# Tiles of x and pieces of the qkv weights in one packed array, and an order made with other costs of transfers

## The chip, the core and the metric

The kernel runs on one core of a Trainium2 chip. The metric is the time of one execution on the device in microseconds (us). Besides PE (TensorE: matmuls, and the loads of their stationary operand, PEld), the core has DVE (VectorE), ACT (ScalarE), POOL (GpSimd) and SP (SyncE), which here issues every DMA. Each engine runs its own list of instructions in the order in which it was built; an instruction that waits holds up all that stand behind it on its engine.

## What is computed

```python
def _A_ref(x, wqkv, wo):                      # linear attention, 32 heads of 16
    q, k, v = split_heads(x @ wqkv)
    phi = lambda t: where(t > 0, t + 1, exp(t)) + 1e-6
    pq, pk = phi(q), phi(k)
    kv = einsum("bhsd,bhse->bhde", pk, v)
    z = einsum("bhsd->bhd", pk)
    num = einsum("bhqd,bhde->bhqe", pq, kv)
    den = einsum("bhqd,bhd->bhq", pq, z)[..., None] + 1e-6
    return merge_heads(num / den) @ wo
def _B_ref(x, w_gate, w_up, w_down):
    return (gelu(x @ w_gate) * (x @ w_up)) @ w_down

xn = layernorm(x)
return x + _A_ref(xn, wqkv, wo) * silu(_B_ref(xn, w_gate, w_up, w_down))
```

x is 2048 tokens by 512, the inner width of the feed-forward part is 1792, everything is in 32-bit floats.

## The kernel before

A 32-bit product is made of three fast ones: each operand is split into a high part (a cast on ACT) and a low part (the difference, on DVE or POOL), and PE sums high x high, high x low and low x high (`sum3`, whose matmuls all carry line 506 in the profile; the splits carry 484 and 490). The large products use seven block products in place of eight, so sums of blocks are formed first, mostly on POOL.

The stages: up to 145 us, layer normalisation, q and k (`plain` for the first two pairs of tiles, then `first_products` and `rest`) and the sum G of xn by phi(k) (`gps`); then the feed-forward part for the second 1024 tokens, with the splits of all weights on the way (139 to 345 us); the small products that give one matrix per head; the feed-forward part for the first 1024 tokens, with the queries' normalisation in between (`queries`: tiles q, u, ptq, pT, then stored as pn_d); and from about 560 us the product S with these queries (read back as `pb`), the gate and the output.

**The start.** x comes in tiles of 128 tokens, 256 KB each, `x0`, `x4`, `x1`, `x5` and so on (`load_x`, L589), in a ring of four buffers. The array is row-major, so such a tile lies in one piece in memory. The weights of q, k and v lie as [3, 128, 4, 512]: a piece [1, :, k] of 256 KB is 128 rows of 2 KB, 8 KB apart. `wk1` and `wk2` are two pieces each of k's weights, `wq1` and `wq2` of q's, `wv` of v's. A tile of x gets statistics (`st`, L644; `mv`, L645; `ve`, L647, all DVE), the root on POOL (`rstd`, L649), the normalised tile (`xn`, L653, DVE), four transpositions on PE (`pt`, L675) and then on ACT a copy (`xt`) and the high parts `Xh` (L484); DVE makes `Xl`. The weights become `kq` (casts on ACT, low parts on DVE, for wk2 on POOL). PE starts with 13 warm-up matmuls, then the transposition of x0, then `k` products; `fill` are matmuls without use that stand in the order where PE might wait.

**What sets the order.** Every operation is recorded by `do` with its engine and a cost in microseconds; a DMA also with its size (`dma`, L458). `Plan` replays the record with these costs: it gives each transfer a time on one shared queue (its way there, its bytes by RATE, its landing), runs the engines against each other in 14 rounds, and each round takes the operations by the due times that the round before gave. The last round's order is what is built. So any cost that is changed can move instructions on all engines, while the set of instructions stays the same.

Eight DMAs can be under way at a time: a ninth waits until the first has landed, and so on.

Of the kernel before, what the change touches and what calls it, by code (L numbers as in the profile page):

```python
# [71 lines left out]
class Op:  # L72
    __slots__ = ("eng", "cost", "fn", "pre", "suc", "key", "name", "port", "kb", "n", "out", "use")


class Plan:

    RATE = 365.0
    TAIL = {"PE": 0.19, "ACT": 0.13, "DVE": 0.12, "POOL": 0.07, "SP": 0.0}
    HEAD = {"PE": 0.14, "ACT": 0.01, "DVE": 0.01, "POOL": 0.04, "SP": 0.05}  # L80
    SAME = {"ACT": 0.15, "DVE": 0.13, "POOL": 0.09}
    LAND = 1.3
    SLOW, FULL = 1.3, 6.0
    WAY = 0.45
    BEGIN = 0.65
    ROUNDS = 14
    MARGIN = (0.1, 0.12, 1.0)
# [7 lines left out]

    def do(self, eng, cost, fn, out, *ins, more=(), key=None, name="", kb=0):
# [7 lines left out]
        op.pre, op.suc, op.kb = set(), [], kb  # L104
# [36 lines left out]
    def hop(self, p, s):  # L141
        if p.eng == "SP":
            return self.LAND + (0.0 if s.eng == "SP" else self.HEAD[s.eng])
        if p.eng == s.eng:
            return self.SAME.get(p.eng, 0.0) if set(p.out) & set(s.use) else 0.0
        return self.TAIL[p.eng] + self.HEAD[s.eng]

    def link(self, pe_keys, to_pe, to_all, landing):
# [10 lines left out]
        self.behind = [[(p.n, lag(p, o)) for p in o.pre] for o in self.ops]  # L159
        self.info = [(o.eng, o.cost, o.port, o.kb / self.RATE) for o in self.ops]  # L160
        chain = [list(row) for row in self.ahead]
# [4 lines left out]
    def tails(self, nxt):  # L166
# [16 lines left out]
        for i in reversed(topo):  # L183
            _, cost, _, move = self.info[i]
            late[i] = min([late[j] - lag for j, lag in nxt[i]], default=0.0) - cost - move
        return late

    def run(self, nxt, late):
# [3 lines left out]
        for row in nxt:  # L192
            for j, _ in row:
                left[j] += 1
        free = dict.fromkeys(self.TAIL, self.BEGIN)
        coming = {e: [] for e in free}
        here = {e: [] for e in free}
# [5 lines left out]
        while len(done) < len(nxt):  # L203
# [30 lines left out]
            _, cost, lock, move = info[i]  # L234
            end, t = when + cost, when
# [30 lines left out]
    def replay(self, order):  # L266
# [5 lines left out]
        for i in order:  # L272
            queue[info[i][0]].append(i)
        free = dict.fromkeys(self.TAIL, 0.0)
        port = dma = last = 0.0
        n = 0
        while n < len(order):
# [9 lines left out]
            n += 1  # L287
            _, cost, lock, move = info[pick]
            start[pick] = when
# [3 lines left out]
            if eng == "SP":  # L293
                dma = max(dma, end + self.WAY)
                dma += move * (self.SLOW if dma < self.FULL else 1.0)
                end = dma
            last = max(last, end)
# [77 lines left out]
def kernel(  # L375
    ctx: ExitStack,
    tc: tile.TileContext,
    x: bass.AP,
    xt: bass.AP,
    wqkv: bass.AP,  # L380
    wo: bass.AP,
# [8 lines left out]
    nc = tc.nc  # L390
    S, D = x.shape
    DH = 16
# [64 lines left out]

    def dma(dst, src, kb, name=""):  # L458
        do("SP", 0.475, lambda o, i: nc.sync.dma_start(o, i), dst, src, kb=kb, name=name)

# [118 lines left out]

    tokens = [(8 * (n // 4) + n % 4, 8 * (n // 4) + 4 + n % 4) for n in range(NP)]  # L580

# [22 lines left out]
    for k in range(2):  # L604
        dma(half(wk1, k), ext(wqkv[1, :, k]), 256)
    for k in range(2):
        dma(half(wk2, k), ext(wqkv[1, :, 2 + k]), 256)
    load_next()
    load_next()
    for k in range(2):  # L610
        dma(half(wq1, k), ext(wqkv[0, :, k]), 256)
    for k in range(2):
        dma(half(wq2, k), ext(wqkv[0, :, 2 + k]), 256)
    for k in range(2):
# [139 lines left out]
    def q_out(v, t):  # L754
        dma(q_d(t, slice(t * P, (t + 1) * P)), phi(v, t, "q"), 256)

# [11 lines left out]
    def spill_x(n):  # L768
        for hl in "hl":
            dma(x_d[hl](n, (slice(None), slice(None), n)), xblock(hl, 0, 7, n).map(lambda ap: ap.bitcast(F32)), 896)  # L770

# [143 lines left out]
    for c in range(KT):  # L915
        g = U("p", range(18, 21), f"GTa{c}")
        copy("DVE" if c % 2 else "ACT", g, gps[c], D, "GT")
        dma(g_d(c, (slice(None), c)), g, 256)

# [44 lines left out]
    def keep_weights(key, ws):  # L964
        w_d[key] = []
        for g, w in enumerate(ws):
            n = GROUPS[g].stop - GROUPS[g].start
            d = dram_view([P, 2, n, P], f"{key[0]}{key[1]}{g}_d")(0, slice(None))
            dma(d, w.map(lambda ap: ap.bitcast(F32)), 128 * n)
            w_d[key].append(d)  # L970
# [19 lines left out]
    def prep_w(p, q):  # L990
# [5 lines left out]
        if p:  # L996
            u, i = divmod(q, 2)
            raw = D2(ring("raw", RAW), f"raw{q}", F32, (P, KT, 2 * P), 1)
            dma(raw, ext((w_up if i else w_gate)[u]), 512)
# [8 lines left out]
    def prep_d(p, u):  # L1008
        ws = wdn[p, u] = weights("D", u, f"wd{u}")
        if p:  # L1010
            raw = D2(ring("raw", RAW), f"draw{u}", F32, (P, 2, D), 1)
            dma(raw, ext(w_down[u]), 512)
            make_weights(ws, raw, D_BLOCKS, f"wd{u}")
# [125 lines left out]
    def queries(i):  # L1139
# [26 lines left out]
        j = t0 % 8  # L1166
        dma(pn_d[0 if t0 < 8 else 1](j // 2, (slice(None), slice(None), slice(j * P, (j + 2) * P))), pTs, 512)

# [34 lines left out]
    def attn_loads():  # L1203
# [73 lines left out]
    for n, key in enumerate(KEYS):  # L1277
        dma(g1_d(n, n), acc[1, key], 256)
    for a in range(2):
# [56 lines left out]
    def s_quad(p, c, forms, g, xp):  # L1336
# [12 lines left out]
        def block(dh, th, e, ps, to):  # L1349
# [14 lines left out]
            for h in range(m):  # L1364
# [4 lines left out]
                if not p:  # L1369
                    dma(ext(out[k * P:(k + 1) * P, lo:lo + w]), x, w // 2)  # L1370
            if p:
                left[k] = left.get(k, 2) - 1
                if not left[k]:
                    dma(ext(out[k * P:(k + 1) * P, HALF:2 * HALF]), o, 512)

# [19 lines left out]
    def x_again(p):  # L1395

        got = {}
        for k in (0, 2, 1, 3):
            got[k] = tile_in("dp", ring("br", BR), [P, HALF], F32, f"xp{p}{k}", 4)
            dma(got[k], ext(xt[k * P:(k + 1) * P, p * HALF:(p + 1) * HALF]), 512)  # L1400
        return got
# [29 lines left out]
def laid_out(inputs, shape):  # L1431
# [36 lines left out]
```

## Time and profile before

| | us |
|---|---|
| median of 3 runs (lowest, highest) | 605.5 (604.25, 607.61) |
| profiled execution | 608.37 |
| its span | 606.7 |
| PE busy in the span | 596.6 |
| DVE, POOL, ACT busy | 486.5, 353.1, 337.2 |

The profile is of one execution. Its span begins with the first and ends with the last instruction; 1.7 us of its time lie outside. Matmuls follow each other every 0.227 us (twelve in 2.72 us) but are shown 0.39 us long, since their ends overlap, so an idle PE shows, and a PE that runs at half clock shows only in the granted clock.

### The profile page before, as it was taken

Reading aid. Unit: us, or ns where it says so; the run is one execution under the profiler, and the core shown is the slowest. Engines: PE = TensorE matmul, PEld = TensorE weight load, DVE = VectorE, ACT = ScalarE, POOL = GpSimd, SP = SyncE. Lnnn points to the kernel's source line nnn. Section 1 sums busy time; section 2 is a strip of 40 time slices with the busy share of each in tenths; the row PEclk is TensorE's granted clock in tenths of the full one; section 3 lists DMA queues with packets and bytes.
Section 4 is the critical chain, followed back from the end, with each engine's and each line's share of the span. In section 5 each row is a group of like instructions: output and inputs, shape, how many; then the busy total and the mean of one; then the engine's idle time right before and its main releaser. Section 6 shows DMA issues by size and latency. Waiting matters only on the chain.

```text
span 606.7 us, 8238 instructions
## 1 busy us (share of the span) xinstructions
PE 596.6 (98%) x2696; PEld 490.5 (81%) x2696; DVE 486.5 (80%) x700; ACT 337.2 (56%) x610; POOL 353.1 (58%) x298
## 2 busy tenths in 40 slices
PE   7999999999999999999999999999999999999996
PEld 6888888888888888888887878888888888887875
DVE  5898888976598988998979764668865795689997
ACT  5767777786576744665365154645403540477831
POOL 4713854464487975996587234547604670658455
PEclk9999999999999999999999999999999999999999
DMA  7267811219849746973659979988639774899546
GB/s 242 78 209 232 281 70 58 94 54 352 324 149 328 245 180 229 352 256 123 231 177 382 377 231 413 408 285 294 203 126 316 256 240 142 311 298 335 180 139 242
DMA packets 58794, 143.14 MB, mean 236 GB/s; under 512 B 5504, under 2 KB 17024, under 8 KB 58752
## 3 DMA queue, kind: packets, MB, share of 16 engines
q1 hardware_dynamic: 58752, 142.63, 67.0%
q8 instruction: 21, 0.34, 0.3%
q14 instruction: 21, 0.17, 0.1%
HBM read 81.00 MB, written 61.60 MB: 235 GB/s over the span
## 4 chain that ended last, share of the span: by engine, by line
PE 92%; DMA 4%; DVE 3%; ACT 1%; issue 0%; SPq 0%; DVEq 0%; ACTq 0%
PE FX L506 24%; PE FZ L506 12%; PE DX L506 12%; PE gps L506 7%; PE FY L506 6%; PE DZ L506 6%; PE X L506 5%; PE SX L506 4%; PE Z L506 3%; PE DY L506 3%; PE SZ L506 2%; PE k L506 2%; PE q L506 2%; DMA pb<-pn_d 2%; PE Y L506 1%; PE ptq L1163 1%
## 5 line engine op out<-in xcount | busy, mean ns | idle before, releaser
L506 PE MATMUL FX<-Xh,w 128*128 128x512 f32 x448 | 151.7, 390 | 0.0
L1071 POOL TENSOR_TENSOR h<-h,g 128x512 f32<-128x512 f32 x42 | 64.5, 1540 | 92.3 <-DVE h L490 88.5
L506 PEld LDWEIGHTS FX<-Xh,w 128*128 128x128 f32 x448 | 83.9, 188 | 17.3
L490 POOL TENSOR_TENSOR h<-h,h 128x512 f32<-128x512 f32 x56 | 84.2, 1504 | 13.5 <-DVE hf4l L490 3.4
L506 PE MATMUL FX<-Xl,w 128*128 128x512 f32 x224 | 87.3, 390 | 0.0
L506 PE MATMUL FZ<-Xh,w 128*128 128x512 f32 x224 | 78.2, 391 | 0.0
L484 ACT COPY fu<-FX 128x512 f32<-128x512 f32 x56 | 32.9, 588 | 72.3 <-PE FX L506 60.5
L506 PE MATMUL gps<-pks,xns 128*128 128x512 f32 x192 | 49.4, 390 | 0.0
L506 PEld LDWEIGHTS FX<-Xl,w 128*128 128x128 f32 x224 | 42.0, 188 | 8.8
L506 PEld LDWEIGHTS FZ<-Xh,w 128*128 128x128 f32 x224 | 41.7, 188 | 8.7
L751 POOL TENSOR_TENSOR zacc<-zacc,kp 128x512 f32<-128x512 f32 x16 | 24.1, 1507 | 38.8 <-DVE kp L740 38.3
L1097 DVE TENSOR_TENSOR acc<-acc,DX 128x512 f32<-128x512 f32 x48 | 32.5, 683 | 14.8 <-PE DX L506 14.5
L506 PE MATMUL FZ<-Xl,w 128*128 128x512 f32 x112 | 43.7, 390 | 0.0
L506 PEld LDWEIGHTS gps<-pks,xns 128*128 128x128 f32 x192 | 36.0, 188 | 7.6
L506 PE MATMUL FY<-Xh,w 128*128 128x512 f32 x112 | 39.5, 393 | 0.0
L1097 DVE TENSOR_TENSOR acc<-acc,DZ 128x512 f32<-128x512 f32 x32 | 21.8, 681 | 12.6 <-PE DZ L506 8.8
L506 PE MATMUL X<-kq,Xh 128*128 128x512 f32 x96 | 31.1, 398 | 0.0
L490 DVE TENSOR_TENSOR h<-fu,FZ 128x512 f32<-128x512 f32 x28 | 19.2, 684 | 14.8 <-ACT fu L484 8.5
L1063 ACT ACTIVATE g<-g 128x512 f32<-128x512 f32 x42 | 26.6, 632 | 7.7 <-DVE g L490 7.5
L490 DVE TENSOR_TENSOR w<-raw,w 128x512 fp32r<-128x512 f32 (+1 forms) x28 | 24.9, 892 | 3.9 <-ACT w L484 3.9
L490 POOL TENSOR_TENSOR u<-q,zacc 128x512 f32<-128x512 f32 x16 | 22.2, 1404 | 9.8 <-DMA q<-q_d 9.8
L484 ACT COPY fe<-FX 128x512 f32<-128x512 f32 x28 | 16.4, 587 | 20.3 <-PE FX L506 17.0
(422 smaller groups left out, 1604.7 us busy)
## 6 DMA issues: line engine op xcount, KB each, us to landing
w_d<-w SPq DMA_DIRECT2D x36, 512.0 KB, 5.1
w<-w_d SPq DMA_DIRECT2D x36, 512.0 KB, 4.8
wd_d<-wd SPq DMA_DIRECT2D x21, 512.0 KB, 5.0
wd<-wd_d SPq DMA_DIRECT2D x21, 512.0 KB, 6.6
x<-in_x SPq DMA_DIRECT2D x16, 256.0 KB, 5.0
q_d<-qp SPq DMA_DIRECT2D x16, 256.0 KB, 2.0
q<-q_d SPq DMA_DIRECT2D x16, 256.0 KB, 4.3
pn_d<-pT SPq DMA_DIRECT2D x8, 512.0 KB, 6.4
```

The lines of the kernel that those rows point to most:

```text
L484: do("ACT", act(n), lambda o, i: nc.scalar.copy(o, i), dst, src, name=name)
L490: do(eng, c, lambda o, p, q: getattr(e, f"tensor_{op}")(o, p, q), dst, a, b, name=name)
L506: nc.tensor.matmul(o, v[i], v[i + 1], start=start and part == 0 and i == 0, stop=stop and part == 1 and i == len(v) - 2, skip_group_check=on)
L751: do("POOL", pool(D), lambda o, i: nc.gpsimd.tensor_add(o, o, i), zacc, p0, name="zacc")
L1063: curved("gelu", do("ACT", curve(NC), lambda o, i: nc.scalar.activation(o, i, AF.Gelu_apprx_tanh), g, ps if e is None else g, name="gelu"))
L1071: do("POOL", pool(NC), lambda o, i: nc.gpsimd.tensor_mul(o, o, i), h, g, name="h")
L1097: do("DVE", dve(NC), lambda o, i: nc.vector.tensor_add(o, o, i), a, ps, name="acc")
L1163: nc.tensor.transpose(o[:, k, :], a[:, k * P:(k + 1) * P], b)
```

## The change

The host stacks the sixteen tiles of x and the twelve pieces of wq, wk and wv into one array `in_first` of [28, 128, 512], each piece in one stretch of 256 KB, in the order FIRST: x0, wk1's two, x4, wk2's two, x1, x5, the four of q, the other tiles of x, the four of v. The kernel loads piece PLACE of it where it loaded from `in_x` or `in_wqkv`. Sizes, buffers and the count of DMAs stay.

The costs of transfers in `Plan` are replaced: in place of one way (0.45) and landing (1.3), RATE 365 and a factor of 1.3 in the first 6 us, there are four kinds with a way, a landing and a gap that is added to the transfer's time, and RATE 400. The kind "first" is given to the loads of the other weights and of x's transposed copy, "store" and "pieces" to stores. SP begins at 0.85 in place of 0.65. By that all engines get another order.

```diff
+PAIRED = [(8 * (n // 4) + n % 4, 8 * (n // 4) + 4 + n % 4) for n in range(8)]
+XS = [t for pair in PAIRED for t in pair]
+FIRST = [XS[0], ("k", 0), ("k", 1), XS[1], ("k", 2), ("k", 3), XS[2], XS[3], *[("q", k) for k in range(4)], *XS[4:], *[("v", k) for k in range(4)]]
+PLACE = {v: i for i, v in enumerate(FIRST)}
...
-    RATE = 365.0
+    RATE = 400.0
+    MOVES = {"load": (0.72, 0.8, 0.0), "first": (0.72, 0.8, 0.7), "store": (0.45, 0.43, 0.0), "pieces": (0.45, 0.43, 0.6)}
-    LAND = 1.3
-    SLOW, FULL = 1.3, 6.0
-    WAY = 0.45
     BEGIN = 0.65
+    ISSUE = 0.85
...
+        op.way, op.land, gap = self.MOVES[kind]
+        op.kb = kb / self.RATE + gap if kb else 0.0
...
         if p.eng == "SP":
-            return self.LAND + (0.0 if s.eng == "SP" else self.HEAD[s.eng])
+            return p.land + (0.0 if s.eng == "SP" else self.HEAD[s.eng])
...
             if eng == "SP":
-                dma = max(dma, end + self.WAY)
-                dma += move * (self.SLOW if dma < self.FULL else 1.0)
-                end = dma
+                end = dma = max(dma, end + way) + move
...
-        dma(xs[t], ext(x[t * P:(t + 1) * P, :]), 256)
+        dma(xs[t], ext(first[PLACE[t]]), 256)
...
-        dma(half(wk1, k), ext(wqkv[1, :, k]), 256)
+        dma(half(wk1, k), ext(first[PLACE["k", k]]), 256)
...
-            dma(half(wv[c // 2], c % 2), ext(wqkv[2, :, c]), 256)
+            dma(half(wv[c // 2], c % 2), ext(first[PLACE["v", c]]), 256)
...
+    def piece(v):
+        if isinstance(v, tuple):
+            c = d * "qkv".index(v[0])
+            return wqkv[v[1] * P:(v[1] + 1) * P, c:c + d]
+        return x[v * P:(v + 1) * P]
     arrays = {
-        "in_x": x,
+        "in_first": np.stack([piece(v) for v in FIRST]),
...
-        "in_wqkv": wqkv.reshape(d // P, P, 3, d).transpose(2, 1, 0, 3),
```

**ACT at the start**, before: the first instructions behind the load of its table. (pt0 is the transposition of x0, pt4 that of x4, a21 a high part of wq1.)

```order
L484 CAST kq0_221<-wk1_182 128x512 x2
L484 CAST xns0_233<-xn0_223 128x512
L484 COPY xt0_245<-pt0_235 128x512
L484 CAST Xh0_253<-pt0_235 128x256
L484 CAST kq0_221<-wk2_201 128x512
L484 CAST Xh0_253<-pt0_235 128x256
L484 CAST kq0_221<-wk2_201 128x512
L484 CAST a2100_273<-wq1_210 128x512
L484 CAST xns4_283<-xn4_275 128x512
L484 COPY xt0_245<-pt4_285 128x512
```

The same place now:

```order
L486 CAST kq0_216<-wk1_194 128x512 x2
L486 CAST xns0_232<-xn0_222 128x512
L486 CAST kq0_216<-wk2_201 128x512
L486 COPY xt0_251<-pt0_238 128x512
L486 CAST Xh0_255<-pt0_238 128x256 x2
L486 CAST kq0_216<-wk2_201 128x512
L486 CAST a2100_269<-wq1_214 128x512
L486 CAST a2101_277<-wq1_214 128x512
L486 CAST xns4_288<-xn4_281 128x512
L486 COPY xt0_251<-pt4_291 128x512
```

The cast of wk2's first piece moved ahead of the copy and of both casts of x0's transposition, and the cast of wq1's second piece ahead of xns4.

**DVE at the start**, before: from the statistics of x4 to the root's argument for x1 and x5.

```order
L644 BN_STATS st4_240<-x4_199 128x6
...
L490 TENSOR_TENSOR kq0_221<-wk1_182,kq0_221 128x512
L490 TENSOR_TENSOR Xl0_265<-pt0_235,Xh0_253 128x256
L644 BN_STATS st1_267<-x1_204 128x6
L653 TENSOR_SCALAR xn4_275<-x4_199,mv4_248,rstd4_257 128x512
L644 BN_STATS st5_279<-x5_208 128x6
...
L647 TENSOR_SCALAR ve1_299<-mv1_293 128x2
```

The same place now:

```order
L646 BN_STATS st4_234<-x4_199 128x6
...
L492 TENSOR_TENSOR kq0_216<-wk1_194,kq0_216 128x512
L646 BN_STATS st1_259<-x1_206 128x6
L492 TENSOR_TENSOR Xl0_267<-pt0_238,Xh0_255 128x256
L646 BN_STATS st5_271<-x5_208 128x6
...
L655 TENSOR_SCALAR xn4_281<-x4_199,mv4_245,rstd4_257 128x512
...
L646 BN_STATS st2_296<-x2_230 128x6
L647 BN_AGGR mv2_301<-st2_296 128x2
L649 TENSOR_SCALAR ve1_305<-mv1_279 128x2
```

The statistics of x1 and x5 moved ahead of Xl0 and xn4, and those of x2 ahead of ve1.

**ACT where the feed-forward part ends** and S begins, before: pT6 is the last transposition of the queries, stored as pn_d and loaded again as pb; hf0h are high parts of the last unit, which PE needs for DX and DZ.

```order
L484 COPY fu3_1_5236<-FX1_5128 128x512
L484 CAST Xh0_253<-pb100_5192 128x512
L484 COPY pT6_5201<-ptq7_5182 128x4x128
L476 ACT_TABLE_LOAD
...
L484 CAST hf0h_5216<-h12_1_5278 128x512
L1130 ACTIVATE g1_5_5274<-g1_5_5274 128x512
L484 CAST Xh0_253<-pb110_5297 128x512
L484 CAST hf0h_5216<-h22_1_5246 128x512
L484 CAST hf0h_5216<-h21_1_5262 128x512
```

The same place now:

```order
L486 COPY pT6_5222<-ptq7_5200 128x4x128
L486 COPY fu3_1_5237<-FX1_5126 128x512
L486 CAST Xh0_255<-pb100_5214 128x512
...
L486 CAST Xh0_255<-pb110_5269 128x512
L1132 ACTIVATE g1_5_5264<-g1_5_5264 128x512
L486 CAST hf0h_5216<-h12_1_5277 128x512
L1132 ACTIVATE g1_6_5288<-g1_6_5288 128x512
L486 CAST hf0h_5216<-h22_1_5247 128x512
L1132 ACTIVATE g1_7_5307<-g1_7_5307 128x512
L486 CAST hf0h_5216<-h21_1_5271 128x512
```

The copy of pT6 moved two places up, and the cast of pb110 ahead of the cast of h12. On PE the last product, a half of X before, is Z now.

More of the change, by code (lines that the diff above doesn't have):

```diff
@@ L94, in __init__, with do @@
         self.first = 0
-    def do(self, eng, cost, fn, out, *ins, more=(), key=None, name="", kb=0):
+    def do(self, eng, cost, fn, out, *ins, more=(), key=None, name="", kb=0, kind="load"):
         op = Op()
@@ L195, in run @@
         free = dict.fromkeys(self.TAIL, self.BEGIN)
+        free["SP"] = self.ISSUE
         coming = {e: [] for e in free}
@@ L233, in run @@
                 continue
-            _, cost, lock, move = info[i]
+            _, cost, lock, move, way = info[i]
             end, t = when + cost, when
@@ L274, in replay @@
         free = dict.fromkeys(self.TAIL, 0.0)
+        free["SP"] = self.ISSUE
         port = dma = last = 0.0
@@ L287, in replay @@
             n += 1
-            _, cost, lock, move = info[pick]
+            _, cost, lock, move, way = info[pick]
             start[pick] = when
@@ L293, in replay @@
             if eng == "SP":
-                dma = max(dma, end + self.WAY)
-                dma += move * (self.SLOW if dma < self.FULL else 1.0)
-                end = dma
+                end = dma = max(dma, end + way) + move
             last = max(last, end)
@@ L377 @@
     tc: tile.TileContext,
-    x: bass.AP,
+    first: bass.AP,
     xt: bass.AP,
-    wqkv: bass.AP,
     wo: bass.AP,
@@ L578, in kq_split @@
                 split(kq(slot, 0, i), kq(slot, 1, i), raw[:, i], D, f"kq{slot}", eng)
-    tokens = [(8 * (n // 4) + n % 4, 8 * (n // 4) + 4 + n % 4) for n in range(NP)]
+    tokens = PAIRED
     def half(v, i):
@@ L604 @@
     for k in range(2):
-        dma(half(wk1, k), ext(wqkv[1, :, k]), 256)
+        dma(half(wk1, k), ext(first[PLACE["k", k]]), 256)
     for k in range(2):
-        dma(half(wk2, k), ext(wqkv[1, :, 2 + k]), 256)
+        dma(half(wk2, k), ext(first[PLACE["k", 2 + k]]), 256)
     load_next()
@@ L610 @@
     for k in range(2):
-        dma(half(wq1, k), ext(wqkv[0, :, k]), 256)
+        dma(half(wq1, k), ext(first[PLACE["q", k]]), 256)
     for k in range(2):
-        dma(half(wq2, k), ext(wqkv[0, :, 2 + k]), 256)
+        dma(half(wq2, k), ext(first[PLACE["q", 2 + k]]), 256)
     for k in range(2):
@@ L1166, in queries @@
         j = t0 % 8
[L1167 removed]
+        dma(pn_d[0 if t0 < 8 else 1](j // 2, (slice(None), slice(None), slice(j * P, (j + 2) * P))), pTs, 512, "pieces")
     PAIRS = {2: [0], 3: [1], 4: [2], 5: [], 6: [], 7: [3], 8: [4], 9: [5], 10: [], 11: [6], 12: [7]}
@@ L1277 @@
     for n, key in enumerate(KEYS):
-        dma(g1_d(n, n), acc[1, key], 256)
+        dma(g1_d(n, n), acc[1, key], 256, "store")
     for a in range(2):
@@ L1369, in block @@
                 if not p:
-                    dma(ext(out[k * P:(k + 1) * P, lo:lo + w]), x, w // 2)
+                    dma(ext(out[k * P:(k + 1) * P, lo:lo + w]), x, w // 2, "store")
             if p:
@@ L1373, in block @@
                 if not left[k]:
-                    dma(ext(out[k * P:(k + 1) * P, HALF:2 * HALF]), o, 512)
+                    dma(ext(out[k * P:(k + 1) * P, HALF:2 * HALF]), o, 512, "store")
         left = {}
```

28 lines of the change are left out of this document (14 added, 14 removed).

## The prediction

> **What bounds the kernel now.** I read the page's busy table and then the windows: start and end of a stretch, its length, busy time of PE, PE's weight loads, DVE, ACT and POOL (with instruction counts), the granted PE clock, the DMA share and GB/s.
>
> ```profile
> PE 596.6 (98%) x2696; PEld 490.5 (81%) x2696; DVE 486.5 (80%) x700; ACT 337.2 (56%) x610; POOL 353.1 (58%) x298
> ```
> ```profile
> 0.00:15.00 15.00, 11.17 (x54) 9.74 (x55) 8.75 (x21) 7.92 (x15) 6.01 (x12) 0.95 0.72 245
> 15.00:30.00 15.00, 14.94 (x72) 12.35 (x71) 12.54 (x23) 11.27 (x22) 12.10 (x12) 0.94 0.24 72
> 30.00:45.00 15.00, 15.00 (x70) 12.35 (x70) 14.39 (x26) 10.45 (x17) 2.69 (x2) 1.00 0.64 211
> ...
> 315.00:330.00 15.00, 14.60 (x65) 11.71 (x64) 13.82 (x17) 7.43 (x15) 11.70 (x10) 1.00 0.99 364
> 330.00:345.00 15.00, 14.99 (x72) 12.25 (x71) 12.78 (x21) 4.01 (x7) 6.83 (x7) 1.00 1.03 405
> ...
> 540.00:555.00 15.00, 14.32 (x64) 11.43 (x63) 12.94 (x16) 9.39 (x17) 13.85 (x9) 1.00 0.97 328
> ```
>
> PE is the bound. Of the span of 606.7 us it is idle for 10.1: 3.83 in the first 15 us, 0.06 in the next, 0.40, 0.01 and 0.68 in the three late stretches shown, and the rest, 5.1, behind the last matmul. The matmuls themselves are not touched, so only four things can move: the start, the clock in it, the two small holes, and the end. The first is the largest, so I read it in order of time (start, duration, engine, line, operation, and in brackets the wait before it and what ended it).
>
> ```profile
> 3.55 0.70 DVE L644 BATCH_NORM_STATS2 st<-x 128x6 f32<-128x512 f32 x1 [2.45 <-DMA x<-in_x]
> 4.99 0.62 ACT L484 CAST kq<-wk 128x512 fp32r<-128x512 f32 x1 [2.91 <-DMA wk<-in_wqkv]
> 6.74 0.62 ACT L484 CAST kq<-wk 128x512 fp32r<-128x512 f32 x1 [1.14 <-DMA wk<-in_wqkv]
> 7.46 0.69 DVE L644 BATCH_NORM_STATS2 st<-x 128x6 f32<-128x512 f32 x1 [0.98 <-DMA x<-in_x]
> 9.28 0.62 ACT L484 CAST kq<-wk 128x512 fp32r<-128x512 f32 x1 [0.64 <-DMA wk<-in_wqkv]
> 9.98 2.51 POOL L490 TENSOR_TENSOR kq<-wk,kq 128x512 fp32r<-128x512 f32 x2 [0.38 <-DMA wk<-in_wqkv]
> 11.99 0.62 ACT L484 CAST a<-wq 128x512 fp32r<-128x512 f32 x1 [1.29 <-DMA wq<-in_wqkv]
> ```
>
> Each row starts when its tile lands, so these are the landings of x0, both pieces of wk1, x4, both pieces of wk2, and the first of wq1 (x1 and x5 lie between the last two). The steps are 1.44, 1.75, 0.72, 1.82, 0.70 and 2.01 us; the last is for three tiles, 0.67 each. Every tile has 256 KB, so three of the steps hold an extra 0.8 to 1.1 us, about 3 us together, and all three are steps to a wk piece. The windows show the same hole in the traffic:
>
> ```profile
> 2.50:3.50 1.00, 1.00 (x7) 1.00 (x7) 0.00 (x0) 0.00 (x0) 0.00 (x0) 1.00 0.90 342
> 3.50:5.00 1.50, 1.50 (x9) 1.50 (x9) 1.03 (x3) 0.01 (x1) 0.27 (x1) 1.00 0.50 119
> ...
> 8.50:12.00 3.50, 1.92 (x6) 0.97 (x6) 2.46 (x5) 1.56 (x5) 2.98 (x3) 1.00 1.04 396
> 9.75:13.25 3.50, 1.38 (x8) 0.91 (x8) 3.03 (x4) 2.01 (x5) 2.51 (x2) 1.00 0.79 301
> 13.25:16.75 3.50, 3.50 (x13) 2.82 (x11) 3.42 (x10) 2.11 (x6) 2.47 (x4) 0.52 0.28 85
> ```
>
> 342 GB/s, then 119 for 1.5 us with the transfer engines half busy; from 8.5 us on 396. The last two rows show the second loss: PE works 1.38 of 3.50 us, and in the next 3.50 us its clock is 0.52, which costs 0.48 x 3.50 = 1.7 us. What PE waited for is here:
>
> ```profile
> 6.73 0.60 PE L675 MATMUL pt<-ident,xn 128*128 128x128 f32 x4
> 8.27 0.37 ACT L484 CAST Xh<-pt 128x256 fp32r<-128x256 f32 x1
> 8.64 0.96 POOL L649 TENSOR_TENSOR rstd<-ve,neg_half 128x1 f32<-128x1 f32 x1 [3.35 <-DVE ve L647]
> 9.81 0.37 ACT L484 CAST Xh<-pt 128x256 fp32r<-128x256 f32 x1
> 11.26 1.52 DVE L653 TENSOR_SCALAR xn<-x,mv,rstd 128x512 f32<-128x512 f32 x1
> 12.83 0.44 PE L675 MATMUL pt<-ident,xn 128*128 128x128 f32 x2 [1.18 <-DVE xn L653]
> 16.23 1.82 PE L506 MATMUL k<-kq,b 128*128 128x512 f32 x6
> 17.89 0.60 PE L675 MATMUL pt<-ident,xn 128*128 128x128 f32 x4
> ```
>
> **The change, part by part.** *Packing.* It removes no bytes and no DMA: the first twelve tiles stay 256 KB each, issued by SP in nearly the same order. What can change is the spacing. Upper end: nothing, the hole belongs to the first microseconds of any traffic. Lower end: every step is 0.67 us. For the first speaks that the wq pieces, cut with the same stride, run in the 396 GB/s row. For the second speaks that all three long steps end in wk, the first pieces of in_wqkv to be read, while x4, 1 MB further on in the array that x0 had opened, comes in 0.72: the hole looks like the price of opening a second array, and the packed array is opened once, by x0. I take the second. Landings are then 3.55 + n x 0.68: wk1 at 4.2 and 4.9, x4 5.6, wk2 6.3 and 7.0, x1 7.6, x5 8.3, wq1 9.0, three microseconds before 11.99.
>
> The Trainium skill speaks against this: Perfetto Trace Analysis, section "Contiguity and DMAs", says that contiguity matters for a transfer only within a partition's line. The lines are 2 KB before and after, so by that rule packing gives nothing (the first rival). The 396 GB/s row agrees with it; the 119 GB/s row it does not explain.
>
> *The start, with these landings and the new order.* PE's first transposition stays at 6.73, since the 13 warm-up matmuls in front of it remain. ACT now casts wk2's first piece before it empties that transposition: ready at 6.3, cast by 7.0, hidden under the transposition, which ends at 7.33. (With wk2 at 9.28 this same move would hold both Xh casts to about 10.2.) The first k product starts at 8.3 in place of 8.69. Behind it stands x4's path, one step after the other: its statistics follow the split of the first wk piece on DVE, 6.4; POOL's rstd 7.5 to 8.4 in place of 8.64 to 9.60; POOL's two wk2 splits 8.4 to 10.9 (2.51) in place of 9.98 to 12.49. The normalisation xn took 1.52 us and ended 0.29 behind POOL's pair, though x0's took 0.55, so I let it end behind that pair again: 11.2 in place of 12.78. Second transposition: 11.25 in place of 12.83, **term A, -1.6 us**.
>
> From there to the row at 16.23 PE had 3.40 us for four transpositions, six products and a fill, about 2.0 us of work at full clock. If PE's idle share is small enough for the clock to hold, that stretch and the one behind it get back the 1.7 us. By the walk above PE works about 1.8 of the 3.5 us in front of 11.7 (six products and a transposition), against 1.38 of 3.50. Ends: 0 and -1.7. I take **term B, -1.3 us**, nearer to the full gain, since the share rises from 39% to some 50%. The third transposition, at 17.89 in the row, then comes at about 15.0. It needs the statistics of x1 and x5 only, but DVE's new order puts x2's statistics in front: x2 lands at about 11.0, in time.
>
> The Trainium skill, TensorE: Matmul & The Clock Gate, Part 1, has a free-running activity window of about 3.4 us after which an idle PE is halved. The 3.50 us at 0.52 agree; by a free-running window the same start can come out with or without the loss, which is the reason for B's ends.
>
> Does PE keep the 2.9 us? DVE is at 14.39 of 15 us from 30 to 45, so it must come forward too. Its xn of x4 ends 1.6 earlier, and in the stretch from 15 to 30 it is idle for 2.46, most of it behind the slow PE. That covers 2.9.
>
> *The order elsewhere.* From 30 to 315 us PE stands still nowhere. The hole at 540 to 555 is one place:
>
> ```profile
> 548.17 0.62 ACT L484 CAST hf0h<-h 128x512 fp32r<-128x512 f32 x1 [0.23 <-POOL h L490]
> ...
> 550.40 0.62 ACT L484 CAST Xh<-pb 128x512 fp32r<-128x512 f32 x1 [1.07 <-DMA pb<-pn_d]
> 551.60 0.73 PE L506 MATMUL DX<-hf0h,wd 128*128 128x512 f32 x2 [0.68 <-ACT hf0h L484]
> ```
>
> ACT stands at the cast of a loaded tile, two hf0h casts are queued behind it, and PE waits for them. In the new order ACT empties the last transposition of p two instructions earlier, so the store and the load behind it start earlier; but this cast has moved up in front of three hf0h casts. Ends: -0.8 (the hole is gone) and +2.7 (the cast at 548.17, which ran 2.2 us before it, now stands behind it). I take 0, nearest to the row as it is. wv, also packed now, is read at 315 to 340, where PE loses 0.4 us to other things: 0.
>
> *The end.* The last product was half of X, now it is Z. Behind it DVE has three 512-wide operations in place of two and two half ones:
>
> ```profile
> 602.39 0.69 DVE L490 TENSOR_TENSOR xp<-xp,SZ 128x512 f32<-128x512 f32 x1
> 602.99 0.42 DVE L490 TENSOR_TENSOR SX<-acc,SX 128x256 f32<-128x256 f32 x1
> 603.45 0.42 DVE L490 TENSOR_TENSOR xp<-xp,SX 128x256 f32<-128x256 f32 x1
> ```
>
> From Z's last matmul, now 0.8 later, three at about 0.7 end at the same 603.9; the last store has 256 KB, not 128. Ends -0.3 and +0.5; I take 0.
>
> **Sum.** -1.6 - 1.3 = -2.9 us. The profiled execution goes from 608.37 to 605.5 (span 603.8); it lies 2.9 above the median of the runs, 605.5, so the runs go to **602.6**.
>
> **Rivals.** *First: the pieces land as before.* For it: wq with the same stride is fast, and the hole could be the cold start of the queue. Against it: x4's short step. Then neither A nor B comes, and DVE's and ACT's heads wait for x1, x2 and wk2 somewhat longer: 605.5 to 606.5. *Second, slower: ACT's head at 548 to 551.* If the third pb pair lands after about 548.2, when that cast used to run, everything later goes to PE one for one: at the old 550.3 +2.7 us; with the next pair, which stands behind it on the same queue, about +4, and without the gain at the start 609. Against it: the earlier store. *Third: more comes back.* The clock holds entirely, the hole at 550 goes, and the waits of DVE behind 17 us go: -1.6 - 1.7 - 0.8 - 0.5 = -4.6, 600.9.
>
> **How the numbers follow.** Forecast 60%, its own range 600.8 to 604.5; first rival 22%, second 10%, third 8%. 0.5% is 3.0 us, about what a measurement of this kernel can tell from no change; the forecast lies just on that border, so I split it 31 to 29. Faster 31 + 8 = 39%; slower 8 of the second and 1 of the first = 9%; no difference 52%. The range for 8 in 10 leaves out the end of the third and most of the second: 600.0 to 607.0.
>
> **What would show it.** Right: wk2's first piece is cast near 6.5, not 9.28; no window between 3.5 and 8 us under 300 GB/s; the second transposition near 11.3; PE clock 1.00 throughout; the row at 16.23 near 13.5. Wrong at packing: long steps to the wk pieces again. Wrong at A: the wk2 splits on POOL start at 8.4 but xn does not end near 11.2. Wrong at B: a stretch at 0.5 in spite of it. Wrong at "elsewhere": PE idle above 1.5 us between 30 and 600, above all at 548 to 556.

## The result, and the profile after

The changed kernel is slower. The prediction was 602.6 us, within 600.0 to 607.0.

| | before | changed |
|---|---|---|
| median of 7 runs each, us | 605.75 (604.25 to 607.61) | 610.26 (608.78 to 612.88) |
| ratio to before, 95% interval | | 1.0072 (1.0047 to 1.0098) |
| profiled execution, its span | 608.37, 606.7 | 612.25, 610.5 |
| PE busy in the span | 596.6 | 597.8 |

The start came out nearly as forecast, and more than that was lost later. In the order of time, the first casts of weights, POOL's pair of wk2 splits, the second transposition, the row that stood at 16.23 and the third transposition, from the timeline of the changed kernel (start, duration, engine, line, operation, the wait before it and what ended it; lines are two higher than before):

```profile
4.31 0.62 ACT L486 CAST kq<-wk 128x512 fp32r<-128x512 f32 x1 [2.23 <-DMA wk<-in_first]
5.12 0.62 ACT L486 CAST kq<-wk 128x512 fp32r<-128x512 f32 x1 [0.20 <-DMA wk<-in_first]
7.12 0.62 ACT L486 CAST kq<-wk 128x512 fp32r<-128x512 f32 x1 [0.46 <-DMA wk<-in_first]
...
8.63 2.52 POOL L492 TENSOR_TENSOR kq<-wk,kq 128x512 fp32r<-128x512 f32 x2
11.50 0.66 PE L677 MATMUL pt<-ident,xn 128*128 128x128 f32 x4 [1.08 <-DVE xn L655]
13.61 1.54 PE L508 MATMUL k<-kq,b 128*128 128x512 f32 x6
15.19 0.66 PE L677 MATMUL pt<-ident,xn 128*128 128x128 f32 x4
```

And the windows of the changed kernel, with the columns of the prediction (stretch, length, PE, PEld, DVE, ACT, POOL busy, granted clock, DMA share, GB/s):

```profile
3.50:5.00 1.50, 1.50 (x9) 1.50 (x9) 1.03 (x3) 0.62 (x1) 0.14 (x1) 1.00 0.93 309
0.00:15.00 15.00, 12.61 (x62) 10.81 (x62) 10.39 (x25) 9.94 (x19) 7.05 (x14) 1.00 0.74 245
15.00:30.00 15.00, 14.90 (x75) 12.37 (x75) 14.25 (x26) 10.92 (x22) 13.08 (x11) 1.00 0.31 97
330.00:345.00 15.00, 12.71 (x60) 10.70 (x59) 9.72 (x15) 1.76 (x4) 3.60 (x5) 0.89 0.92 359
375.00:390.00 15.00, 13.60 (x64) 11.04 (x64) 9.02 (x12) 5.32 (x10) 8.40 (x7) 1.00 1.02 407
390.00:405.00 15.00, 14.66 (x64) 11.42 (x64) 12.20 (x20) 8.97 (x17) 5.36 (x4) 1.00 0.93 340
405.00:420.00 15.00, 14.61 (x72) 11.99 (x70) 8.97 (x13) 7.79 (x14) 9.31 (x7) 1.00 0.82 274
```

The hole of 119 GB/s is gone, PE works 1.4 us more in the first 15 us and keeps its clock: the third transposition comes 2.70 us earlier. The loss is in two places in which the kernel before had no such wait: 330 to 345 us, where PE is idle for 2.29 us and then has a lower clock, and 375 to 420 us, idle for 2.13, where PE of the kernel before was busy for all of the 45 us. What PE waited for, in the same timeline:

```profile
337.63 0.38 PE L1250 MATMUL pkv<-GT,wv 128*128 128x128 f32 x2
338.68 0.49 PE L1250 MATMUL pkv<-GT,wv 128*128 128x128 f32 x2 [0.67 <-DMA GT<-g_d]
340.68 5.37 PE L1250 MATMUL pkv<-GT,wv 128*128 128x128 f32 x28 [1.51 <-DMA wv<-in_first]
...
387.04 0.66 PE L1165 MATMUL ptq<-ident,q 128*128 128x128 f32 x4 [1.40 <-DVE q L1159]
```

`pkv` are the 32 kv products: per head, GT (the sum G) by wv. In the kernel before they ran without a wait:

```profile
343.84 3.73 PE L1248 MATMUL pkv<-GT,wv 128*128 128x128 f32 x32
```

They now take from 337.63 to 346.05, 8.42 us in place of 3.73: 4.7 us. The loads of wv did not get slower (median from issue to landing 7.4 us, 7.5 before); those of GT took 0.9 us more (9.7, 8.8 before). The second pair of wv was issued 3.1 us earlier than before (first the row of the kernel before, then of the changed one), but the products stand 6.2 us earlier:

```profile
335.47 0.93 SPq L459 DMA_DIRECT2D wv<-in_wqkv  x2
```
```profile
332.33 0.96 SPq L461 DMA_DIRECT2D wv<-in_first  x2
```

About half of the 6.2 us is that PE arrives earlier, the other half is the new order: by the count of PE's matmuls in front of the first product (in brackets behind PE's busy time), 1525 stood there and now 1512, 13 fewer, and 13 x 0.227 = 3.0 us. First the kernel before, then the changed one:

```profile
0.00:343.83 343.83, 339.53 (x1525) 280.43 (x1526) 291.62 (x426) 217.09 (x398) 218.94 (x202) 1.00 0.61 217
```
```profile
0.00:337.62 337.62, 335.09 (x1512) 276.69 (x1513) 286.31 (x419) 216.03 (x398) 220.52 (x202) 1.00 0.61 217
```

At 387 us it is the same on a longer path: the queries' transposition waits for DVE, DVE for POOL, and POOL for the load of q, issued 3.6 us later than before (372.18, was 368.60), while PE gets there 0.9 us later (385.64, was 384.70). First the transposition in the kernel before, without a wait, then the load and POOL in the changed one:

```profile
384.70 0.60 PE L1163 MATMUL ptq<-ident,q 128*128 128x128 f32 x4
```

```profile
372.18 1.08 SPq L461 DMA_DIRECT2D q<-q_d  x2
...
381.29 2.54 POOL L492 TENSOR_TENSOR u<-q,zacc 128x512 f32<-128x512 f32 x2 [7.16 <-DMA q<-q_d]
```

The hole at 548 to 556 us that the prediction watched became no larger: 0.68 us of idle PE before, 0.41 now. The end, from the start of the last matmul to the end of the span, went from 5.4 to 5.7 us.

### The profile page after: what moved, and what is told of

Same layout as the page of the kernel before. It is cut to its first block, busy times and chain, and to the rows that moved or that the text cites. A ratio compares the mean times of both kernels' runs of the same rounds, so it can differ in the third digit from the quotient of the medians.

```text
span 610.5 us, 8231 instructions
## 1 busy us (share of the span) xinstructions
PE 597.8 (98%) x2696; PEld 490.8 (80%) x2696; DVE 483.3 (79%) x700; ACT 335.6 (55%) x610; POOL 354.0 (58%) x298
## 4 chain that ended last, share of the span: by engine, by line
PE 80%; DMA 10%; DVE 5%; POOL 2%; ACT 1%; issue 1%; SPq 0%; POOLq 0%; DVEq 0%; ACTq 0%
PE FX L508 21%; PE DX L508 11%; PE FZ L508 10%; PE gps L508 7%; PE X L508 5%; PE DZ L508 5%; PE FY L508 5%; PE Z L508 3%; DMA q<-q_d 2%; PE DY L508 2%; PE SX L508 2%; PE q L508 2%; DMA GT<-g_d 2%; DMA x<-in_first 1%; DMA wv<-in_first 1%; PE Y L508 1%
## 5 line engine op out<-in xcount | busy, mean ns | idle before, releaser
L492 DVE TENSOR_TENSOR g<-fu,FZ 128x512 f32<-128x512 f32 x28 | 19.0, 680 | 8.9 <-ACT fu L486 4.0
```

Of the source, the lines that this page charges most:

```text
L492: do(eng, c, lambda o, p, q: getattr(e, f"tensor_{op}")(o, p, q), dst, a, b, name=name)
```

## The experiments

Each comparison has its own runs of the kernel before beside it, so ratios are compared, and not medians. A percent is 6.1 us.

### The two halves apart

`e1_pack` is the kernel before with the packed array; the planner's costs, and so every engine's order, are the old ones.

```diff
-        dma(xs[t], ext(x[t * P:(t + 1) * P, :]), 256)
+        dma(xs[t], ext(first[PLACE[t]]), 256)
...
-        dma(half(wk1, k), ext(wqkv[1, :, k]), 256)
+        dma(half(wk1, k), ext(first[PLACE["k", k]]), 256)
...
```

> The packed array alone; the costs of transfers in the planner, and so the order of every engine, are those of the kernel before. Theory A (the two halves of the change add: packing gives the start, the order takes it away elsewhere): the pieces land every 0.7 us as in the changed kernel, the third transposition (17.89 us before) comes near 15.5, no wait at the kv products, PE idle from 30 to 600 us stays near 1.1 us: 2 to 2.7 us less than before, 603.0 to 603.8 against 605.75. Rival B (what is gained at the start is given back, since PE then reaches the kv products earlier than their wv pieces can land, the transfers from 312 to 345 us being the limit): a wait of 1 to 3 us for wv at about 341 us, and a time of 605 to 606. Rival C (the fast landings need the new order of the loads too): the landings are as before and the time within 0.5 us of it.

Measured: 604.49 us against 606.31, ratio 0.9972 (0.9954 to 0.9990). `e2_order` is the other half: the changed kernel with the old arrays.

```diff
-        dma(xs[t], ext(first[PLACE[t]]), 256)
+        dma(xs[t], ext(x[t * P:(t + 1) * P, :]), 256)
...
```

> The new costs of transfers alone, with x and the qkv weights in their old two arrays; every engine has the order of the changed kernel. Theory A: all of the loss (some 6.5 us) and none of the gain at the start, and the wk2 cast that now stands ahead of the Xh casts waits for its late piece, up to 1 us more: 612 to 613.5 against 610.3 of the changed kernel and 605.75 before; the wait for wv ahead of the kv products is 1 to 2.5 us. Rival B (the loss comes from arriving early): PE comes 2.7 us later to the kv products, their wait for wv is gone, and the time is 607 to 609. Rival C (the gain at the start came with the new order of the loads): the start is as in the changed kernel, 610.

Measured: 613.54 us against 606.31, ratio 1.0123 (1.0091 to 1.0155). In its timeline both faults of the order are there, and one that packing may have covered: PE's first k product waits for Xh and starts at 9.78 us, 1.1 later than in the kernel before (8.69). The cast of wk2's late piece now stands ahead of Xh on ACT, with a wait of 0.36 us and 0.62 of work, which fits; but a second execution of the kernel before, in its old order, starts this product at 9.30, so the cause is not shown.

```profile
9.78 0.97 PE L509 MATMUL k<-kq,Xh 128*128 128x512 f32 x3 [2.37 <-ACT Xh L487]
...
340.45 0.49 PE L1251 MATMUL pkv<-GT,wv 128*128 128x128 f32 x2 [0.56 <-DMA GT<-g_d]
342.46 3.74 PE L1251 MATMUL pkv<-GT,wv 128*128 128x128 f32 x28 [1.51 <-DMA wv<-in_wqkv]
```

Theory A holds, though both times lie above its ranges, `e1_pack` by 0.7 us. Rival C falls: the first wk1 piece is cast at 4.29 us in `e1_pack`, in the old order, and at 5.01 in `e2_order`. Rival B falls: packing alone has no wait at the kv products, though PE reaches them at 340.99 and not at 343.84, and the order alone loses with the late start too. Packing is worth 0.28% with the old order (1.7 us, a little less than expected) and 0.51% with the new one (1.0123 less 1.0072); by the intervals these two do not differ. The order costs 1.0% with packed arrays (1.0072 less 0.9972, 6.1 us), 1.2% without.

### Which cost moved the kv products

`e3_rate` is the changed kernel with one constant put back.

```diff
-    RATE = 400.0
+    RATE = 365.0
```

> The changed kernel with one constant put back: RATE 365 in place of 400; the packed array, the kinds and their landings stay as changed. Theory A, as to which constant: a planner that believes in 400 has the last wv piece landed some 4 us ahead of when it does, and puts the kv products 3.4 us of PE work earlier than before; with 365 they stand where they stood, and the wait of 2.2 us and the half clock behind it (4.4 us together) go: 605 to 606.5, with PE busy over 14.5 of the 15 us from 330 to 345. If the queries at 385 us are healed as well: 603 to 604. Rival D (the shorter landings, 0.8 for 1.3, are what does it): the hole at 337 to 345 us stays, 609.5 to 610.5.

Measured: 606.32 us, ratio 1.0000 (0.9987 to 1.0014): 0.72% less than the changed kernel, 4.4 us. PE has 1527 matmuls in front of the first kv product, 15 more than in the changed kernel, and the wait is gone:

```profile
340.94 3.73 PE L1250 MATMUL pkv<-GT,wv 128*128 128x128 f32 x32
```

PE is busy for 15.00 us from 330 to 345. Rival D, the shorter landings, falls as the sole cause at this place. A wait of 0.99 us for q stays, now near 413 us. `e7_rate400` is the reverse, the kernel before with that constant alone.

```diff
-    RATE = 365.0
+    RATE = 400.0
```

> The kernel before with one constant changed, RATE 400 for 365; arrays and all other costs of transfers as before. The planner then puts the kv products 2.1 us of PE work earlier (in the changed kernel 3.0) and the first transposition of the queries 0.7 us. Theory A (RATE alone places consumers ahead of their loads): PE waits at the kv products, 0.5 to 1.5 us with some half clock behind it, and at the queries near 385 us, 0.5 to 1.5 us: 607.5 to 609.5. Rival D (it takes the shorter landings too): no wait above 0.5 us at either place, and 605.8 to 606.8.

Measured: 612.88 us (610.45 to 615.62), ratio 1.0105 (1.0074 to 1.0137). It lies above the range of either theory. Its profile (an execution of 615.62) has waits in many places, by the table of PE's waits (what PE waited for, us in total, times, longest):

```profile
PE k L506 <- ACT Xh L484: 2.1, 1, 2.1
PE pt L675 <- DVE xn L653: 1.7, 1, 1.7
PE FX L506 <- ACT fu L484: 1.6, 1, 1.6
...
PE pkv L1248 <- DMA wv<-in_wqkv: 0.6, 1, 0.6
```

The wait for wv is there, 0.6 us as expected, with 1516 matmuls in front of the first kv product, but it is the smaller part: the first two rows are a late start (its second wk1 piece was cast at 8.46 us, from the same place in SP's order as before), and 1.6 us at 155 us were not expected at all. So RATE alone is enough to make the kernel slower, and to bring a wait at the kv products; that these waits make up the loss is shown for the changed kernel only. RATE alone moves the products by 9 matmuls in place of 13, and the 28 products behind its wait take 3.75 us, with no half clock: the other new costs have a part in the size of the changed kernel's loss there.

### How much each place is worth

`e4_late` leaves the new costs but gives a longer landing to the eight loads of GT and wv.

```diff
-    MOVES = {"load": (0.72, 0.8, 0.0), ...}
+    MOVES = {"load": (0.72, 0.8, 0.0), ..., "late": (0.72, 5.0, 0.0)}
...
-            dma(gt[c], g_d(c, (slice(None), c)), 256)
+            dma(gt[c], g_d(c, (slice(None), c)), 256, "late")
...
-            dma(half(wv[c // 2], c % 2), ext(first[PLACE["v", c]]), 256)
+            dma(half(wv[c // 2], c % 2), ext(first[PLACE["v", c]]), 256, "late")
```

> The changed kernel with a longer landing in the planner (5.0 for 0.8 us) for eight loads alone, the four of GT and the four of wv. The kv products then stand 4.8 us of PE work later. Theory A: the wait at the kv products was one of place alone; it goes with its half clock, 4.4 us, while the waits near 385 us (2.4 us) stay: 605.5 to 607. Rival E (the transfers from 312 to 345 us are the bound, so that whatever PE puts in front waits as well): the hole moves by some us and stays over 2 us, and the time is 609 to 610.5.

Measured: 607.32 us, ratio 1.0009 (0.9992 to 1.0025): 0.63% less than the changed kernel, 3.8 us. The products start at 342.69 and take 3.73 us again, the wait at the queries stays:

```profile
342.69 3.73 PE L1250 MATMUL pkv<-GT,wv 128*128 128x128 f32 x32
...
382.63 0.55 PE L1165 MATMUL ptq<-ident,q 128*128 128x128 f32 x3 [1.42 <-DVE q L1159]
```

The transfers were not the bound; PE had other work for the time, and only stood in front of the wrong one. (A new cost changes the order elsewhere too, so the 3.8 us need not be of this place alone.) `e8_late_q` gives the long landing to the loads of q too.

```diff
-            dma(half(q, n), q_d(t, slice(t * P, (t + 1) * P)), 256)
+            dma(half(q, n), q_d(t, slice(t * P, (t + 1) * P)), 256, "late")
```

> The changed kernel with the long landing (5.0 us) for the loads of GT, wv and, in addition to the run before, of the queries q; their first transposition then stands 4.1 us of PE work later. Theory A (the waits at the queries are the same fault, a consumer placed ahead of its load): the waits of 1.58 and 0.52 us near 381 and the one of 0.54 us at 414 us go, 604.8 to 605.8 against 607.3. Rival F (the load is late because SP stands at another load whose buffer is not free, and every later place only moves with it): a wait of over 1 us stays, 607.

Measured: 606.21 us, ratio 1.0002 (0.9988 to 1.0016). The first queries now run without a wait, and one of 0.40 us at 468 us is left:

```profile
385.01 1.03 PE L1165 MATMUL ptq<-ident,q 128*128 128x128 f32 x8
```

So the waits went, as theory A has it, and the span of the profiled execution fell by 1.8 us (605.9 to 604.1); but the median lies above theory A's range, the two ratios differ by 0.07% with intervals of 0.15% on either side, and the runs do not show what this second place is worth. Nor do they show where the 0.3% between this kernel and `e1_pack` lies: its largest waits in PE behind the start are the 0.40 us and one of 0.33 us, and a sum of small differences at the start and the end is as far as the profiles go.

### What made the steps long

Two kernels in the old order separate the stride from the second array. `e5_contig` keeps two arrays and lays the weights out so that each piece is in one stretch:

```diff
-        "in_wqkv": wqkv.reshape(d // P, P, 3, d).transpose(2, 1, 0, 3),
+        "in_wqkv": wqkv.reshape(d // P, P, 3, d).transpose(2, 0, 1, 3),
...
-        dma(half(wk1, k), ext(wqkv[1, :, k]), 256)
+        dma(half(wk1, k), ext(wqkv[1, k]), 256)
```

> The kernel before, every engine in its old order, x and the qkv weights in two arrays as before; only the weight array is laid out as [3, 4, 128, 512], so that each 256 KB piece lies in one stretch. Theory P (what the prediction took: the long steps are the price of the first reads of a second array): landings as before, wk1 at 4.99, wk2 at 9.28, wq1 at 11.99 us, and a time within 0.1% of before, 606.3. Theory S (the 8 KB stride of the pieces is what makes the steps long): every step about 0.7 us, wk2 near 7.1, wq1 near 10, as with the packed array, and its time, 604.5.

Measured: 605.12 us against 606.89, ratio 0.9979 (0.9963 to 0.9995). `e6_one` puts both into one array, with the pieces 8 KB apart as before:

```diff
-        "in_x": x,
+        "in_both": np.concatenate([x, wqkv.reshape(d // P, P, 3, d).transpose(2, 1, 0, 3).reshape(-1, d)]),
...
+    x = both[:S]
+    wqkv = both[S:].rearrange("(t p k) n -> t p k n", t=3, p=P)
```

> The kernel before in its old order, with x and the qkv weights in one array, x first and the weights behind it in their old layout, so that the pieces keep their 8 KB stride. Theory P (a second array): the long steps go, wk2 near 7.1 us, 604.5. Theory S (the stride): landings as before, wk2 near 9.3, 606.3. If both this and the kernel with contiguous pieces in two arrays keep the long steps, then it takes the two together, or the place of a piece right behind the one before it.

Measured: 606.03 us, ratio 0.9997 (0.9977 to 1.0018). The window of the first wk1 piece and its cast, first of `e5_contig`, then of `e6_one`:

```profile
3.50:5.00 1.50, 1.50 (x9) 1.50 (x9) 0.98 (x3) 0.62 (x1) 0.36 (x1) 1.00 0.83 229
...
4.07 0.62 ACT L484 CAST kq<-wk 128x512 fp32r<-128x512 f32 x1 [1.99 <-DMA wk<-in_wqkv]
```
```profile
3.50:5.00 1.50, 1.50 (x9) 1.50 (x9) 1.03 (x3) 0.00 (x0) 0.23 (x1) 1.00 0.42 117
...
5.35 0.62 ACT L485 CAST kq<-wk 128x512 fp32r<-128x512 f32 x1 [3.27 <-DMA wk<-in_both]
```

It is the stride that makes the first pieces late, by these landings; the two times alone would not tell, since their intervals overlap. Two arrays with contiguous pieces have the first piece as early as the packed one, one array with strided pieces as late as the kernel before. All other profiles agree: the first wk1 piece is cast at 4.07 to 4.31 us in the eight with contiguous pieces and at 4.99 to 5.35 in the five with strided ones, the second at 5.92 at the latest against 6.74 at the earliest. But not every step is 0.7 us, as theory S had it: the second wk1 piece comes 1.73 us behind the first in `e5_contig` and 1.54 in `e1_pack`, much as in the kernel before (1.75), and only 0.81 in the changed one. What makes this step long is open.

A late piece need not become a late start. In the execution of `e6_one`, PE's second transposition comes at 11.27 us, earlier than in `e1_pack` (11.65):

```profile
11.27 0.66 PE L676 MATMUL pt<-ident,xn 128*128 128x128 f32 x4 [0.23 <-DVE xn L654]
```

### Two kernels once more, and the best of both

`e10_before_again` and `e11_pack_again` are the kernel before and `e1_pack` once more, with nothing changed.

```diff
+# again
```

> The kernel before once more, for a second profile of it. In 10 of 58 executions of it the mean granted clock was 0.993 to 0.996 and their median 608.4 us, against 606.3 in the 34 with 0.998 to 1.000; the profile on which the prediction rests is one of the 10. If the half clock from 13 to 17 us (1.7 us) is what tells them apart, this execution has it when its mean clock is under 0.997, and else a clock of 1.00 there and a span some 2 us shorter, 604 to 605. The hole of 119 GB/s and the late first wk piece (4.99 us) are there in both cases.

> The packed array with the old order once more, for a second profile of it: how far the start of one and the same kernel differs from execution to execution. By the median of its runs (604.5) the span should be 602 to 603.7. The first wk piece lands at 4.1 to 4.4 us and the clock stays at 1.00 to 30 us, as in all profiles of kernels with contiguous pieces so far.

The first took 607.04 us (span 605.3, mean clock 0.997), the second 603.84 (span 602.1, 0.999). Windows, first of the kernel before again, then of the packed one again:

```profile
3.50:5.00 1.50, 1.50 (x13) 1.50 (x13) 0.98 (x3) 0.00 (x0) 0.36 (x1) 1.00 0.63 154
...
9.75:13.25 3.50, 3.21 (x12) 2.13 (x11) 3.14 (x9) 2.31 (x6) 3.21 (x4) 0.65 0.91 322
13.25:16.75 3.50, 3.50 (x19) 2.94 (x17) 2.65 (x6) 2.81 (x7) 3.41 (x4) 0.86 0.28 81
```
```profile
3.50:5.00 1.50, 1.50 (x9) 1.50 (x9) 1.03 (x3) 0.72 (x2) 0.20 (x1) 1.00 1.33 232
...
13.25:16.75 3.50, 3.50 (x22) 2.83 (x21) 3.10 (x5) 3.19 (x7) 3.34 (x5) 1.00 0.35 105
```

The loss of clock at the start of the kernel before comes at another time here, from about 11 us, and the span is 1.4 us shorter than in the execution that the prediction used, though with a hole (154 GB/s) and a late first wk1 piece (5.14) again. The second transposition comes 1.04 us earlier than there (12.83), with nothing changed:

```profile
11.79 1.06 PE L675 MATMUL pt<-ident,xn 128*128 128x128 f32 x4
```

By its mean clock it was expected to have 1.00 there and a span of 604 to 605; both were missed, so the half clock is not at one fixed place, and 0.997 is no clean border. The mean clock also falls by half clock at the very end, where PE has no work: `e4_late` has a mean of 0.997 with a clock of 1.00 up to 602 us, its last matmul starts at 600.22, and then

```profile
602.00:605.00 3.00, 0.00 (x0) 0.00 (x0) 1.01 (x2) 0.00 (x0) 0.00 (x0) 0.63 0.74 264
```

The packed kernel kept its clock, as expected, and its two spans differ by 1.6 us.

`e9_pack_slow1` is `e1_pack` with the planner told that the first transfers are not slow, which gives the start nearly the changed kernel's order.

```diff
-    SLOW, FULL = 1.3, 6.0
+    SLOW, FULL = 1.0, 6.0
```

> The packed array with the planner's old costs, less one that the packed start makes untrue: the factor of 1.3 on transfers in the first 6 us becomes 1.0. The start then gets nearly the changed kernel's order (the cast of wk2's first piece ahead of both Xh casts, the statistics of x1 and x5 ahead of Xl), and the kv products and the queries keep the place they had before. Theory A with the best of both: 603.5 to 604.5, against 604.5 with the packed array and all old costs. Rival G (any change of these costs stirs the rest of the program: here some 160 rows of PE behind 520 us move too): a new wait of 1 us or more behind 520 us and 605.5 to 606.5.

Measured: 605.75 us against 607.08, ratio 0.9986 (0.9972 to 1.0000). Rival G was nearer, though the wait of 1 us that it named is not there: the start is no worse (PE busy for 9.74 of the first 12 us, 8.98 and 10.43 in the two profiles of `e1_pack`), but PE waits 0.73 us for a copy on ACT at 595 us and 0.46 us for a cast at 547, where `e1_pack` has no wait above 0.24 behind 540 us. The best version remains `e1_pack`, 0.28% below the kernel before and 1.0% below the changed one; `e5_contig` (0.21% below the kernel before) cannot be told from it.

## Why the prediction was wrong

**What bounds the kernel** was right: PE has no slack, and all that could be traced came and went as idle time and clock of PE.

**Packing** was right in its direction and wrong in its reason. wk1 was forecast at 4.2 and 4.9 and came at 4.31 and 5.12; wk2, forecast at 6.3, came at 7.12, and wq1, forecast at 9.0, at 9.99, so the even steps of 0.68 us were too short by 0.8 to 1.0 us in all. The hole was put down to the opening of a second array; `e6_one` has one array and the hole. What led there was x4's short step; but x4 is itself a piece in one stretch, so that step fits the stride as well. The wq pieces, with the same stride at 396 GB/s, only show that the stride costs nothing once the first microseconds are over. The rule that the prediction weighed against packing (the Trainium skill, Perfetto Trace Analysis, "Contiguity and DMAs": contiguity matters for a transfer only within a partition's line) does not hold here for the first pieces: the lines are 2 KB in `e5_contig` as before, and the first piece comes 0.9 us earlier. For wv at 315 to 340 us the trace agrees with it: median landing 7.5 us strided and 7.4 contiguous.

**Term A**, -1.6, was near in this pair of profiles: the second transposition came at 11.50, 1.33 us earlier (11.25 forecast), behind the steps that were forecast (POOL's pair from 8.63 us, 8.4 forecast). How much of that is packing's is not shown: the kernel before has this transposition at 12.83 in one execution and at 11.79 in the other, `e1_pack` at 11.65 and 10.51. The median with packing alone fell by 1.7 us, but in the old order and with all that packing does, so that its agreement with the -1.6 is luck.

**Term B**, -1.3, is in the profile (clock 1.00 in place of 0.95 and 0.94) but can be in the median only in part. In 15 of 75 executions of the kernel before the mean granted clock was 0.996 or less, and their median was 608.35 us; in the 43 with 0.998 or more it was 606.31. The profiled execution, with 0.995, was one of the 15. The prediction's sum, -2.9, was then set against the median, where most executions do not have the loss that B gives back. This is a first step that failed, the last sentence of the sum: the 2.9 us between this execution and the median were carried over as a constant, and by the two medians some 2.0 of them go with the low clock. In the 72 timed executions of the six other packed or contiguous kernels no mean clock is under 0.997, while 3 of 12 of `e6_one` are. So B is a loss that packing ends, but one that only some executions have: at least one in five, and more if others with 0.997 are like `e10_before_again`, which had it. That an idle PE costs clock at differing times agrees with the free-running window of the Trainium skill (TensorE: Matmul & The Clock Gate, Part 1): 0.52 from 13.25 us in one execution, 0.65 from 9.75 in another. No wait of PE ahead of these losses was longer than 1.9 us.

**The order elsewhere**, 0, is the step that decided, and it failed: a term that was put at nothing. It looked at one hole that the kernel before had, and there little changed (0.68 to 0.41 us, but 0.2 in the second execution of the kernel before). It dismissed wv "at 315 to 340, where PE loses 0.4 us to other things": the prediction's own row for 330 to 345 had a DMA share of 1.03, and the kv products stood 8.4 us behind the issue of the last wv pair, with landings of 7.4 to 8.0 us. That is 342.9 to 343.5 for the first of the pair, a slack of about half a microsecond at the old place, and PE's new order has them 3.0 us of work earlier: an estimate of 2.5 us of waiting, which the trace of the kernel before and the two orders allowed. Measured: 4.7 us there in the profile, of which the products at half clock are 2.1 (28 in 5.37 us, 3.3 at full clock), and 3.8 in the runs (`e4_late`). The queries, 2.1 us of idle PE, were not in the sum at all. By the ratios, packing's -1.7 us and the order's +6.1 make +4.4, and +4.5 was measured; of the 6.1, the 2.3 beside the kv products are traced to no place.

**The second rival** had the right kind of loss, a load that lands behind the new place of its consumer, at the wrong place, ACT's head at 548 us, and with 10%. Its price for one place, 2.7 to 4 us, was near to what the kv products cost. The first and third rivals: the pieces did not land as before, and the clock did hold entirely at the start, but the rest of the third did not follow.

**The end**, 0, measured +0.3, inside its ends.

## What to carry to other kernels

When a planner's costs change, go through every place where PE's next operand comes straight from a load, take the row where the load was issued and its measured landing, and compare the slack with how many rows its consumer moved; here a rate of 400, near the most that the stretches above show (405 and 407 GB/s), made an order that stands in front of loads. Judge the pieces of a change apart: here the data layout gained 0.3% and the new costs that came with it lost 1.0%. A loss seen in one profiled execution counts against the median only as often as it occurs, and a row that shifts by 1 us between two executions of one kernel cannot by itself show a term of that size; the mean clock of the single runs gives a hint of how often a clock loss occurs, no more.

## What the runs showed of the hardware

- 256 KB pieces of 128 rows of 2 KB that lie 8 KB apart: 117 to 212 GB/s from 3.5 to 5.0 us in the five profiles that have them, against 223 to 347 in the eight with contiguous pieces; from 8.5 to 12 us the strided ones run at 388 to 404 GB/s. Why it is so only at the start was not tried.
- The same kernel with the same order starts differently from execution to execution: in the strided kernels the second wk1 piece was cast anywhere from 6.74 to 8.46 us, and the packed kernel's two spans differ by 1.6 us.
- 2.2 us of waiting at the kv products were followed by half clock in the changed kernel (28 products in 5.37 us) and by none in `e2_order` (3.74 us) after nearly the same wait.
